# Where VectorE takes the largest of the sizes and normalizes pair 14, in a hash attention with a feed-forward behind it

## The chip, the cores and the metric

The kernel runs on one core of one Trainium2 chip. The metric is the time of one execution on the device, in microseconds (us). The kernel before took 877.48 us (median of four runs, 877.30 to 878.19).

The core has a matrix engine (TensorE, PE in the profile, its weight loads PEld), three engines for element-wise work (VectorE, DVE; ScalarE, ACT; GpSimd, POOL), and SyncE (SP), which here only issues DMAs. TensorE writes to PSUM, a small memory in banks; the rest lives in SBUF. The engines run side by side, each through its own list of instructions in order, and wait for one another by semaphores.

## The reference

Attention with a mask made from hashes, then a feed-forward block. Cut to what matters:

```python
# q, k, v: (4, 8, 768, 64) f32; proj: (64, 6); w_in: (512, 2048); w_out: (2048, 512)
q_bucket, k_bucket = bits of (q @ proj > 0), bits of (k @ proj > 0)   # 6 bits as a number
scores = where(q_bucket[..., :, None] == k_bucket[..., None, :], q @ k.T / 8, -1e9)
attn   = exp(scores - max(scores));  attn /= sum(attn) + 1e-9
x      = (attn @ v), heads side by side        # (3072, 512)
h      = x @ w_in
out    = (h * sigmoid(1.702 * h)) @ w_out      # (3072, 512)
```

## The kernel before

**Attention in 16 pairs.** Two heads form a pair, so there are 4 batches x 4 = 16 pairs, numbered 0 to 15 (`last` is 15). For each pair the 768 queries are taken in two halves c = 0 and 1 of 384. `scores(n, c, ...)` (L423) multiplies, for each of 6 tiles of 128 keys, first the hash features and then the keys with the queries (L432, tile ps), and ScalarE takes the exponential into the tile e (L433). The exponentials are taken without the largest score being subtracted first. That is only safe if q and k are not large, and so ScalarE also sums the squares of every pair's q and k (`measure`, L393) into a tile `sizes` with 32 columns. At the end of the kernel every engine loads one number, the largest of the sizes, and a branch (L981 to L984) computes everything anew in a careful way if it is too large.

`guard` (L516) makes this number, in two parts. Part 0 takes on VectorE the largest of the 32 columns in each of 128 partitions (L518). Part 1 turns that column into a row on TensorE (L521, tile row, in the PSUM buffer with the tag m) and takes the largest of the row on VectorE (L522).

**The sum under the softmax.** Each half's 6 tiles of exponentials are added up. `add_low` (L437) adds the first three on GpSimd (L440, L441) into acc0, of which there is one buffer. `add_high` (L443) adds the other three and acc0 on VectorE, by one instruction of L446 and two of L448; the last of them reads acc0. `total` (L472, tile dn) sums both halves over the partitions on TensorE. `invert` (L481) takes reciprocals on VectorE (L485 to L494) and leaves them in the tile rs. `norm` (L497) multiplies a pair's columns of xT by rs (L499), one instruction. `values` (L450, tile av) multiplies exponentials and v on TensorE, and `unload` (L466) brings the result to xT by ScalarE.

**The order.** The four computing engines run in the order in which the program is written (L72, `manual_schedule`). The loop over the pairs (L553 to L593) writes out one pair after another. An iteration n also inverts and normalizes pair n - 1, turns and hashes pair n + 1, and converts a piece of the weight w_in by 6 VectorE instructions (`step(n, 6)`, L178 to L198, with one on ScalarE, L190). In the last iteration there is no next pair: nothing is turned, hashed or measured, and the two parts of `guard` stand there instead. The last lines of the loop's body add `total(n)`, the loads of later pairs, and in the last four pairs one step each of `x_sums` (L219 to L222 on VectorE), which the feed-forward needs.

**Feed-forward in two stages.** Both multiplications are done by Strassen's scheme with 7 products in place of 8. The hidden stage (`hidden`, L698) takes 3 blocks of 1024 tokens by 8 pieces of the hidden dimension; each has 7 products of 4 matmuls (L708), in the order 1, 6, 7, 5, 2, 3, 4. Products 6, 5 and 3 use sums of quarters of w_in (tile s_in), which GpSimd makes (`in_sums`, L211 to L214, directly behind the last pair's add_low in its order). The products' banks in PSUM, six at that time, are read by ScalarE (L720) and VectorE (L721 to L733). The first block of tokens needs batch 0 and a part of batch 1; the columns of pair 14 (batch 3, third pair of heads) are used from the third block on. The hidden values go to memory and come back for the second stage (L820), whose result is turned (L800) and written out.

Of the kernel before, what the change touches and what calls it, by code (L numbers as in the profile page):

```python
# [38 lines left out]
def kernel(  # L39
# [243 lines left out]
    def attention(ff):  # L283
# [4 lines left out]
        with actx:  # L288
# [99 lines left out]
            def turn(n, name):  # L388
                x = raws[n, name]
                xt = xts[n, name] = wk.tile([P, S], F32, tag=f"{name}T", name=f"{name}T")  # L390
                nc.vector.transpose(xt, x.rearrange("p s i -> p (s i)"))
# [10 lines left out]
            def hashed(n):  # L402

                h = dots[n] = mps.tile([P, HS], F32, tag="m", name="hash")
                for i, x in enumerate("kq"):
                    for c in range(2):
                        r0 = D * i + 32 * c
                        nc.tensor.matmul(h[r0 : r0 + 32, :], pf[x], xts[n, x][:, c * HS : (c + 1) * HS],  # L408
                                         start=True, stop=True)

            def featured(n):
                f = wk.tile([P, HS], BF16, tag="f", name="f", bufs=1)
                nc.vector.tensor_scalar(f, dots.pop(n), above[:, 0:1], weight[:, 0:1], op0=Alu.is_gt, op1=Alu.mult)
                for c in range(2):
                    for i, x in enumerate("kq"):

                        queue = nc.scalar if (n, x, c) == (1, "q", 0) else nc.sync
                        for j in range(2):
                            r0 = D * i + 32 * c + 2 * NB * j
                            queue.dma_start(out=feats[n % 2][x][D * j : D * j + 2 * NB, c * HS : (c + 1) * HS],  # L420
                                            in_=f[r0 : r0 + 2 * NB, :])

            def scores(n, c, kts):  # L423
                qT, kT, qf, kf = xts[n, "q"], xts[n, "k"], feats[n % 2]["q"], feats[n % 2]["k"]
                cols = slice(c * HS, (c + 1) * HS)
                for kt in kts:
                    ps = sps.tile([P, 2, 512], F32, tag="s", name="ps")
                    keys = slice(kt * P, (kt + 1) * P)
                    for a, m, last in ((kf, qf, False), (kT, qT, True)):
                        for j in range(2):  # L430
                            hs = slice(D * j, D * (j + 1))
                            nc.tensor.matmul(ps[:, j, 0:HS], a[hs, keys], m[hs, cols], start=not last, stop=last)  # L432
                    nc.scalar.activation(es[c][:, kt, :, 0:HS], ps[:, :, 0:HS], Act.Exp, scale=1.0 / D**0.5)  # L433
# [3 lines left out]
            def add_low(n, c):  # L437

                acc = accs[n, c, 0] = st.tile([P, 2, HS], F32, tag="acc0", name="acc0", bufs=1)
                nc.gpsimd.tensor_tensor(acc, es[c][:, 0, :, 0:HS], es[c][:, 1, :, 0:HS], op=Alu.add)  # L440
                nc.gpsimd.tensor_tensor(acc, acc, es[c][:, 2, :, 0:HS], op=Alu.add)  # L441

            def add_high(n, c):  # L443
                e = [es[c][:, GT + i, :, 0:HS] for i in range(GT)]
                acc = accs[n, c] = st.tile([P, 2, HS], F32, tag="acc", name="acc")
                nc.vector.scalar_tensor_tensor(acc, e[0], T * TINY, e[1], op0=Alu.add, op1=Alu.add)  # L446
                for x in (e[2], accs.pop((n, c, 0))):
                    nc.vector.tensor_tensor(acc, acc, x, op=Alu.add)  # L448

            def values(n, c, kts):  # L450
                if 0 in kts:

                    pool, tag = (mps, "m") if c else (aps, "av")
                    avs[n, c] = pool.tile([P, HS + 1], F32, tag=tag, name="av")
                av, vt = avs[n, c], vts[n]
                for t in kts:
                    for j in range(2):
                        nc.tensor.matmul(av[D * j : D * (j + 1), :], vt[:, t, j, :], es[c][:, t, j, :],  # L458
                                         start=(t == 0), stop=(t == T - 1))

            def x_of(n):
                b, hp = pairs[n]
                x = xT[:, hp, b * S : (b + 1) * S]
                return x.rearrange("d (t p) -> d t p", p=P) if n else x.rearrange("d (p t) -> d t p", p=P)
# [7 lines left out]
            def total(n):  # L472

                dn = accs[n] = aps.tile([P, HS], F32, tag="av", name="dn")
                for c in range(2):
                    acc = accs.pop((n, c))
                    for j in range(2):
                        r0 = D * j + 32 * c
                        nc.tensor.matmul(dn[r0 : r0 + 32, :], ones[:, 0:32], acc[:, j, :], start=True, stop=True)  # L479

            def invert(n):  # L481


                rt = st.tile([P, HS // 32, 32], F32, tag="rt", name="rt", bufs=1)
                nc.vector.transpose(rt.rearrange("p s i -> p (s i)"), accs.pop(n))  # L485
                yield
                r = st.tile([P, 2, HS // 32], F32, tag="r", name="r")
                nc.vector.reciprocal(r, rt[:, :, 0].unsqueeze(1).to_broadcast([P, 2, HS // 32]))
                for r0 in range(0, P, 32):
                    c = r0 // 32 % 2  # L490
                    r1 = r0 + 32 - 64 * c
                    nc.vector.reciprocal(r[r1 : r1 + 32, c], rt[r0 : r0 + 32, :, 0])
                rs = accs[n] = st.tile([P, S], F32, tag="rs", name="rs", bufs=1)
                nc.vector.transpose(rs.rearrange("p (s i) -> p s i", i=32),  # L494
                                    r.rearrange("p c s -> p (c s)").unsqueeze(2).to_broadcast([P, S // 32, 32]))

            def norm(n):  # L497
                x, rs = x_of(n), accs.pop(n)
                nc.vector.tensor_tensor(x, x, rs.rearrange("p (t s) -> p t s", t=T), op=Alu.mult)  # L499

            last = len(pairs) - 1
            conv = {}

            def step(n, count=1):
                for _ in range(count):
                    next(conv.get(n, iter(())), None)
# [9 lines left out]
            def guard(part):  # L516
                if part == 0:
                    nc.vector.tensor_reduce(largest, sizes, axis=AX.X, op=Alu.max)  # L518
                else:
                    row = mps.tile([1, P], F32, tag="m", name="row")  # L520
                    nc.tensor.transpose(row, largest, ident)  # L521
                    nc.vector.tensor_reduce(largest[0:1, 0:1], row, axis=AX.X, op=Alu.max)  # L522
# [30 lines left out]
            for n in range(1, last + 1):  # L553
                scores(n, 0, every)
                add_low(n, 0)
                if n == 1:
                    add_high(0, 1)
                    turn(2, "k")
                    total(0)
                inverted = invert(n - 1)  # L560
                next(inverted)
                if 1 < n < last:
                    turn(n + 1, "k")
                whole(inverted)
                scores(n, 1, every)
                add_low(n, 1)
                if n < last:
                    turn(n + 1, "q")
                add_high(n, 0)
                if n < last:  # L570
                    hashed(n + 1)
                    featured(n + 1)
                    for x in "kq":
                        measure(n + 1, x)
                else:
                    guard(0)
                    guard(1)
                norm(n - 1)
                add_high(n, 1)
                values(n, 0, every)  # L580
                unload(n, 0)
                step(n, 6)
                values(n, 1, every)
                unload(n, 1)
                total(n)
                if n + 2 <= last:
                    for x in "kq":
                        fetch(n + 2, x)
                if n < last:
                    fetch_v(n + 1)  # L590
                    begin(n + 1)
                if n > last - len(x_sums):
                    x_sums[n - last - 1]()  # L593
# [378 lines left out]
    def whole(steps):  # L972
        for _ in steps:
            pass

    ff = feed_forward("", in_chunks[len(in_chunks) - LATE :])
    attention(ff)
    whole(ff)
    fixed.close()
# [41 lines left out]
```

## Time and profile before

| what | value |
|---|---|
| median of 4 runs | 877.48 us (877.30 to 878.19) |
| the profiled execution's own time | 877.48 us |
| its span, first to last instruction | 875.7 us |
| TensorE busy | 862.6 us (99%) |
| VectorE busy | 719.0 us (82%) |
| GpSimd busy | 321.3 us (37%) |
| ScalarE busy | 312.0 us (36%) |
| granted TensorE clock, mean | 0.998 |
| last pair, from its first score product to dn | 302.95 to 322.49 us |
| hidden stage | 323.3 to 611.9 us |
| second stage, TensorE's steady part | 611.9 to 850.6 us |
| behind it, to the end | 25.1 us |

All times in the views count from the first instruction of the span. A line of a timeline gives the start, the duration, the engine, the line of the program, the operation, the tile written and the tiles read; idle time before it is in brackets, with what ended it. Consecutive instructions of the same kind are merged, with x for their number. A TensorE product's end is modelled, so that successive products overlap a little. The chain is followed back from the last instruction, at each step to what released it.

### The profile page before, as it was taken

The numbers are of one execution on the slowest core, as the hardware profiler recorded it, in microseconds if no ns is written. First come the engines' busy times: TensorE is split into PE (matmuls) and PEld (weight loads), VectorE is DVE, ScalarE is ACT, GpSimd is POOL, SyncE is SP. The second block draws the span as 40 slices with busy tenths as digits, with TensorE's granted clock in tenths as the row PEclk, the third lists the DMA queues.
The fourth block names the chain that finished last, engine by engine and source line by source line (L and its number), as shares of the span: only waits on it lengthen the run. The fifth ranks groups of instructions, "written<-read, shape, count | busy, mean of one in ns | idle before, by whom it ended". The sixth has DMA issues, their size and how long they took to land.

```text
span 875.7 us, 11818 instructions
## 1 busy us (share of the span) xinstructions
PE 862.6 (99%) x4077; PEld 501.7 (57%) x4077; DVE 719.0 (82%) x1020; ACT 312.0 (36%) x519; POOL 321.3 (37%) x275
## 2 busy tenths in 40 slices
PE   9999999999999999999999999999999999999995
PEld 5444444444444444444444444444888888888884
DVE  4479999988999997788777787888888977897785
ACT  5766577777666643222232222332000000000000
POOL 4244333334433375665443344659903100000000
PEclk9999999999999999999999999999999999999999
DMA  5334456544445304555455645575844685467524
GB/s 130 61 58 84 84 97 106 117 89 83 83 84 91 74 25 144 204 204 200 166 188 190 216 166 202 191 249 171 308 164 159 199 246 198 165 202 241 193 97 99
DMA packets 169155, 131.99 MB, mean 151 GB/s; under 512 B 123616, under 2 KB 138112, under 8 KB 163712
## 3 DMA queue, kind: packets, MB, share of 16 engines
q1 hardware_dynamic: 166528, 129.70, 51.3%
q10 hardware_dynamic: 2560, 1.46, 0.7%
q8 instruction: 34, 0.56, 0.3%
q14 instruction: 33, 0.27, 0.1%
HBM read 79.69 MB, written 50.33 MB: 148 GB/s over the span
## 4 chain that ended last, share of the span: by engine, by line
PE 91%; DVE 6%; issue 1%; DMA 0%; ACT 0%; SPq 0%; ACTq 0%; DVEq 0%
PE product L708 33%; PE product L820 27%; PE ps L432 16%; PE av L458 12%; PE dn L479 1%; DVE acc L448 1%; PE hash L408 1%; DVE acc L446 1%; DVE xT L499 1%; DVE xT L824 1%; PE tp L366 1%; DVE y L800 1%; DMA q<-in_q_dram 0%; DVE t_x L221 0%; PE warm L359 0%
## 5 line engine op out<-in xcount | busy, mean ns | idle before, releaser
L433 ACT ACTIVATE e<-ps 128x768 f32<-128x768 f32 x192 | 150.4, 813 | 16.9 <-PE ps L432 14.6
L432 PE MATMUL ps<-qT,kT 64*128 64x384 f32 x768 | 155.1, 482 | 0.0
L708 PE MATMUL product<-xT,w_in_sb 128*128 128x512 f32 x288 | 135.4, 592 | 0.0
L458 PE MATMUL av<-e,v 128*64 128x385 f32 x768 | 128.2, 488 | 0.0
L440 POOL TENSOR_TENSOR acc<-e 128x768 f32<-128x768 f32 x32 | 50.4, 1575 | 192.8 <-ACT e L433 115.2
L716 ACT ACTIVATE c<-c 128x512 f32<-128x512 f32 x72 | 45.3, 630 | 186.6 <-issue 78.5
L458 PEld LDWEIGHTS av<-e,v 128*64 128x64 f32 x768 | 53.8, 136 | 72.9 <-issue 72.0
L708 PEld LDWEIGHTS product<-xT,w_in_sb 128*128 128x128 f32 x288 | 54.6, 190 | 69.0 <-issue 64.5
L708 PE MATMUL product<-t_x,s_in 128*128 128x512 f32 x192 | 90.2, 592 | 0.0
L432 PEld LDWEIGHTS ps<-qT,kT 64*128 64x128 f32 x768 | 68.1, 187 | 37.8 <-issue 37.4
L219 POOL TENSOR_TENSOR v<-c,u 128x512 f32<-128x512 f32 x24 | 34.2, 1423 | 122.8 <-ACT c L716 122.8
L833 ACT COPY u<-product 128x256 f32<-128x256 f32 x21 | 7.8, 372 | 172.1 <-PE product L820 138.9
L441 POOL TENSOR_TENSOR acc<-acc,e 128x768 f32<-128x768 f32 x32 | 64.0, 2000 | 2.5
L432 PE MATMUL ps<-qf,kf 64*128 64x384 bf16 x384 | 62.9, 324 | 0.1
L708 PEld LDWEIGHTS product<-t_x,s_in 128*128 128x128 f32 x192 | 36.5, 190 | 45.9 <-issue 43.3
L446 DVE SCALAR_TENSOR_TENSOR acc<-e 128x768 f32<-128x768 f32 x32 | 52.1, 1628 | 5.1 <-ACT e L433 5.1
L708 PE MATMUL product<-xT,s_in 128*128 128x512 f32 x96 | 45.1, 592 | 0.0
L708 PE MATMUL product<-t_x,w_in_sb 128*128 128x512 f32 x96 | 45.1, 592 | 0.0
L432 PEld LDWEIGHTS <-kf 64*128 64x128 bf16 x384 | 19.4, 94 | 35.4 <-issue 12.0
L820 PE MATMUL product<-raw_g,xT 128*128 128x256 f32 x152 | 35.1, 379 | 0.0
L448 DVE TENSOR_TENSOR acc<-acc,e 128x768 f32<-128x768 f32 x32 | 31.0, 969 | 3.8 <-ACT e L433 0.5
L448 DVE TENSOR_TENSOR acc<-acc,acc 128x768 f32<-128x768 f32 x32 | 31.0, 969 | 3.3
(207 smaller groups left out, 1495.9 us busy)
## 6 DMA issues: line engine op xcount, KB each, us to landing
raw_g<-g_dram SPq DMA_DIRECT2D x22, 1024.0 KB
s_in<-g_dram SPq DMA_DIRECT2D x20, 1024.0 KB
g_dram<-c SPq DMA_DIRECT2D x72, 256.0 KB
g_dram<-t SPq DMA_DIRECT2D x48, 256.0 KB
raw<-in_moe_w_in_dram SPq DMA_DIRECT2D x16, 512.0 KB
raw<-in_moe_w_out_dram SPq DMA_DIRECT2D x16, 512.0 KB
v<-in_v_dram SPq DMA_DIRECT2D x32, 192.0 KB
g_dram<-u SPq DMA_DIRECT2D x24, 256.0 KB
```

Source lines behind the costliest of these rows:

```text
L219: return [lambda: eng.tensor_tensor(t1, b12, b11, op=Alu.subtract), lambda: eng.tensor_tensor(b12, b22, b12, op=Alu.subtract), lambda: eng ...
L366: nc.tensor.matmul(tp[D * j : D * (j + 1), i * P : (i + 1) * P], x[name][:, j, c * GT + i, :], ident, start=True, stop=True)
L432: nc.tensor.matmul(ps[:, j, 0:HS], a[hs, keys], m[hs, cols], start=not last, stop=last)
L433: nc.scalar.activation(es[c][:, kt, :, 0:HS], ps[:, :, 0:HS], Act.Exp, scale=1.0 / D**0.5)
L440: nc.gpsimd.tensor_tensor(acc, es[c][:, 0, :, 0:HS], es[c][:, 1, :, 0:HS], op=Alu.add)
L441: nc.gpsimd.tensor_tensor(acc, acc, es[c][:, 2, :, 0:HS], op=Alu.add)
L446: nc.vector.scalar_tensor_tensor(acc, e[0], T * TINY, e[1], op0=Alu.add, op1=Alu.add)
L448: nc.vector.tensor_tensor(acc, acc, x, op=Alu.add)
L458: nc.tensor.matmul(av[D * j : D * (j + 1), :], vt[:, t, j, :], es[c][:, t, j, :], start=(t == 0), stop=(t == T - 1))
L708: nc.tensor.matmul(ps, wq[LEFT[i]][:, kc, :], xq[RIGHT[i]][:, kc, :], start=(kc == 0), stop=(kc == K2 - 1))
L716: nc.scalar.activation(c, c, Act.Gelu_apprx_sigmoid)
L820: nc.tensor.matmul(ps, wq[LEFT[i]][:, c, :], gq[RIGHT[i]][:, c, :], start=(c == 0), stop=(c == F4 - 1))
```

## The change

In the last pair's iteration alone, two steps move. `guard(0)`, VectorE's largest over the 32 columns, goes from behind the additions of the first half, add_high(15, 0), to ahead of them and ahead of the scores of the second half. `guard(1)` stays where it was. `norm(14)` goes from ahead of the additions of the second half, add_high(15, 1), to behind them. In all other iterations the order is as before.

```diff
                 whole(inverted)
+                if n == last:
+                    guard(0)
                 scores(n, 1, every)
                 add_low(n, 1)
                 if n < last:
...
                 else:
-                    guard(0)
                     guard(1)
-                norm(n - 1)
+                if n < last:
+                    norm(n - 1)
                 add_high(n, 1)
+                if n == last:
+                    norm(n - 1)
                 values(n, 0, every)
                 unload(n, 0)
                 step(n, 6)
```

VectorE's order in that iteration, before: reciprocals of pair 14, add_high(15, 0), guard(0), guard(1), norm(14), add_high(15, 1), conversion. After: reciprocals of pair 14, guard(0), add_high(15, 0), guard(1), add_high(15, 1), norm(14), conversion.

## The prediction

> **What bounds the kernel now.** I read first the page's busy shares and its chain, then the chain in order of time over the whole run, then the timeline of each engine around the two reductions that the diff moves. The first two say that TensorE is the bound nearly everywhere:
>
> ```profile
> PE 862.6 (99%) x4077; PEld 501.7 (57%) x4077; DVE 719.0 (82%) x1020; ACT 312.0 (36%) x519; POOL 321.3 (37%) x275
> PE 91%; DVE 6%; issue 1%; DMA 0%; ACT 0%; SPq 0%; ACTq 0%; DVEq 0%
> ```
>
> At 99%, a change can only give back time in which TensorE stands still, or make it stand still anew. The chain in order of time (start, duration, what) has such a place next to the edit, at the end of the last pair (pair 15):
>
> ```profile
> 264.46 9.80 PE ps L432 x72
> ...
> 314.22 0.11 DVE largest L518
> 314.37 0.27 PE row L521
> 314.64 7.92 PE av L458 x48
> 322.56 0.78 PE dn L479 x8
> 323.34 288.60 PE product L708 x672
> ```
>
> Up to 314.33 the chain is VectorE's. Then TensorE transposes the column of largest sizes (row, L521), and from there it runs to 850.6 with one hole of 0.11 us (at 689.66). What it gains at 314 it keeps for over 500 us, and the 25.1 us behind, in which VectorE, ScalarE and TensorE take turns, start from its product that ends at 850.6. TensorE's own timeline prices the place; in brackets the idle time before, and what ended it:
>
> ```profile
> 312.01 0.81 PE L432 MATMUL ps<-qT,kT 64*128 64x384 f32 x4
> 314.37 0.27 PE L521 MATMUL row<-ident,largest 128*1 128x128 f32 x1 [1.55 <-DVE largest L518]
> 314.57 7.99 PE L458 MATMUL av<-e,v 128*64 128x385 f32 x48
> 322.49 0.85 PE L479 MATMUL dn<-acc,ones 128*32 128x384 f32 x8
> 323.27 1.98 PE L708 MATMUL product<-xT,w_in_sb 128*128 128x512 f32 x4
> 325.09 1.88 PE L708 MATMUL product<-t_x,s_in 128*128 128x512 f32 x4
> ```
>
> **The change, part by part.** *guard(0) goes ahead of the last pair's additions.* It reads only the sizes. ScalarE's last one was done at 296.2, so it waits for nothing at its new place, right behind the transpose of the reciprocals (L494: 310.27 + 0.98 = 311.25), and ends near 311.4. TensorE comes to the row later than that: its first score product of pair 15 started at 302.95, and in the pairs before the scores took 9.80 (9.79 to 9.84) up to the next kind of product (first line of the second fence), so at 312.75. Its stall was 314.37 - 312.75 = **1.62 us**. The bracket says 1.55, because ends are modelled and successive products overlap by some 0.07. If the change of tile shape cost nothing, the 12 groups at 0.808 would end at 302.95 + 9.69 = 312.64, and the gain would be 1.73. I take 1.62, since all pairs show the 9.80, and keep 1.55 and 1.73 as ends.
>
> Its price: VectorE pays guard(0) (0.18 busy, 0.11 in the chain) ahead of add_high(15,0) and not behind it. I take 0.18: the third addition ends at 314.40, not 314.22. Queued behind that is GpSimd's add_low(15,1), which needs the buffer that this addition reads, and started 0.14 after it: at 314.54 now.
>
> *guard(1) keeps its place on VectorE.* The row now lies ready from 313.0, so VectorE's wait of 0.36 goes, and the reduction (0.28) runs from 314.40 to 314.68. The row's PSUM buffer is wanted again by values(15,1), at half of the 7.92 (316.9): 2.2 us of room. Nothing that is moved issues a DMA, and no step changes its place on the queues of SP, ScalarE or GpSimd.
>
> *norm(14) goes behind add_high(15,1).* VectorE's and GpSimd's timelines:
>
> ```profile
> 314.88 1.83 DVE L499 TENSOR_TENSOR xT<-xT,rs 128x768 f32<-128x768 f32 x1
> 316.64 2.43 DVE L446 SCALAR_TENSOR_TENSOR acc<-e 128x768 f32<-128x768 f32 x1
> 319.18 1.30 DVE L448 TENSOR_TENSOR acc<-acc,e 128x768 f32<-128x768 f32 x1
> 320.58 1.30 DVE L448 TENSOR_TENSOR acc<-acc,acc 128x768 f32<-128x768 f32 x1
> ...
> 314.36 1.54 POOL L440 TENSOR_TENSOR acc<-e 128x768 f32<-128x768 f32 x1 [4.37 <-DVE largest L518]
> 315.98 2.27 POOL L441 TENSOR_TENSOR acc<-acc,e 128x768 f32<-128x768 f32 x1
> 318.22 1.44 POOL L211 TENSOR_TENSOR s_in<-w_in_sb 128x256 f32<-128x256 f32 x1
> 319.74 1.32 POOL L212 TENSOR_TENSOR w_in_sb<-w_in_sb 128x256 f32<-128x256 f32 x1
> 321.03 1.44 POOL L213 TENSOR_TENSOR s_in<-s_in,w_in_sb 128x256 f32<-128x256 f32 x1
> ```
>
> These durations are long: the same L446 took 0.92 for add_high(15,0), and L448 0.96, while GpSimd was quiet, and norm(15) 0.96 where it started first. The Trainium skill (SBUF — State Buffer, "Who interferes with whom") has a rule that speaks against the move: a VectorE instruction with two SBUF inputs and a GpSimd instruction that reads SBUF can't overlap; the one that starts later stands still until the other is done. The rows agree: GpSimd's L440 ends at 315.90 and norm, started under it, at 316.71; L441 ends at 318.25 and L446 at 319.07; L211 at 319.66 and the next L448 at 320.48; L212 at 321.06 and the last L448 at 321.88. They go turn and turn about. Without the rule I would take norm's 1.83 and the 0.36 off the additions, and add the 0.18: 321.88 - 2.01 = 319.87. With it, L446 only takes norm's turn behind L440, and each VectorE turn ends as before plus 0.18: L446 at 316.89, the two L448 at 319.25 and 320.66, norm(14) at 322.06. I take the turns, since they are in the rows.
>
> What depends on it: total(15) (dn) comes forward by 1.62, to 322.49 - 1.62 = 320.87, and its second half, which reads add_high(15,1), some 0.39 later. The sum is there at 320.66: 0.2 to 0.6 us to spare, no wait. This is the cover, and it is thin: with norm still ahead, the sum would come at 321.88 + 0.18 = 322.06, 0.8 behind the second half, and half of the gain would be lost. So the two parts belong together, and the second earns nothing by itself.
>
> Late next: the first feed-forward products. Product 1 (323.27 - 1.62 = 321.65) needs nothing of this. Product 6 (325.09 - 1.62 = 323.47, weights some 0.19 ahead) needs GpSimd's L213, which ended at 322.47 and by the turns now at 322.65: 0.6 to spare. norm(14) is wanted by no product soon: its columns (batch 3, third pair of heads) belong to the last third of the hidden stage, from some 323 + 2/3 x 289 = 515 us. The conversion behind it on VectorE stays within 0.2 of its place, and behind that the sums that free PSUM: product 6 was read at 329.75, and its bank was wanted again at 335.39. The 5.6 less 0.7 for the read leave 4.9; 3.3 after the shift.
>
> **Sum.** The profiled execution took 877.48, of which its span is 875.7 and 1.8 lies around it; the median is also 877.48. -1.62 at the row, 0 at dn, 0 at product 6, nothing given back later: span 874.1, time 877.48 - 1.62 = **875.86 us (-0.18%)**. About 0.2% (1.75 us) is what a measurement of this kernel can tell from no change, so the likeliest gain lies 0.13 us inside that bound.
>
> **The clock** could make it more. The Trainium skill (TensorE: Matmul & The Clock Gate, "What's actually happening") says that the array's clock halves after about one window of 3.4 us without work. A halved clock for one window would make the old gap dearer by 1.7 us, for a total of 3.3. The stages of the windows view show 1.00 granted in the pair with the gap and in the one before, and values(15) took 7.92 as values(14) did, so I count nothing.
>
> **Rivals.**
> (a) *More than the stall.* TensorE loads the row's and the next weights while it still works on scores (the load, 0.08, came after the wait at 314.37), and the shape change is hidden: 1.73 + 0.08 = 1.8, up to 2.1 with what the tail's turns may shift: 875.4 to 875.7. For it: many weight loads run ahead. Against: the 9.80 of every pair includes such loads.
> (b) *A partial gain.* If VectorE's L446 (from 314.65) starts before GpSimd's L440 (from 314.54), the turns are exchanged: L446 ends at 315.5, L440 at 317.0, an L448 at 318.0, L441 at 319.5, L211 at 320.2, the last L448 at 321.1, L212 at 321.8, norm at 322.7, L213 at 323.4. dn just holds, and product 6's weights wait 0.1 to 0.3. With a lost turn more (0.9), the gain is 0.4 to 1.5: 876.0 to 877.1. Only 0.1 us decides which comes first.
> (c) *The hoisted reduction does nothing*, as VectorE comes to it no earlier than TensorE to the row. From 275 VectorE is on the chain, and its lead at the new place is 312.75 - 311.4 = 1.3. Should a load of q land later than the 4.1 us it took at 286.41, each us beyond the 1.3 takes one off the gain: 876 to 877.5. In this trace the lead is whole.
> (d) *Slower.* VectorE's run of two-input steps (three additions, norm, six conversion steps) keeps winning the port, and GpSimd's L213 falls behind by whole turns. Product 6 then waits. From 0.6 + 1.62 = 2.2 us of lateness on, the change loses; over 0.2% it loses from 4.0 us, about four and a half turns of 0.9, at 879.3 or more. Against it: from 314 to 323 the two engines alternate strictly in the trace.
>
> **How the numbers follow.** Full gain, 1.55 to 1.73: 0.70. Medians repeat to about 0.2 us (three of the four times lie between 877.30 and 877.50), and the bound is 0.13 away, so I put 0.36 within and 0.34 beyond it. (a): 0.12, faster. (b) and (c): 0.09, within. (d): 0.09, slower. Faster 0.46, same 0.45, slower 0.09. The range: from (a)'s 875.4, less 0.1 of scatter, to 877.0, which takes in most of (b) and (c) and leaves out (d).
>
> **What would show it.** L518 near 311.3; no idle time before the row, which starts at 312.75; guard(1) with no wait; L446 of add_high(15,1) from 314.7 with about 2.2 us, norm(14) from 320.7; dn at 320.87, the first product at 321.65, the hidden products 288.6 us as before, and a span of 874.1. A wait of TensorE for L448 at dn, or for L213 at product 6, would show (b) or (d). Idle time left before the row would show (c).

## The result, and the profile after

The changed kernel took **875.72 us** (median of 36 runs, 874.92 to 878.74), against 877.10 (median of 57, 876.07 to 878.62) for the kernel before, measured beside it. The ratio is 0.9984 with a 95% interval of 0.9979 to 0.9988: 0.16% faster, just inside the 0.2% that the prediction called the bound of a measurement. The forecast was 875.86. That the time itself fits to 0.14 us is in part luck: the forecast took its 1.62 off the 877.48 of four runs, and the kernel before, measured beside the changed one, came out at 877.10. From there 1.62 less would be 875.48; the measured gain is 1.38.

TensorE no longer stands at the row. From the changed kernel's chain in order of time (start, duration, what), over the same stretch as before:

```profile
302.74 9.80 PE ps L432 x72
312.54 0.20 PE row L521
312.74 7.92 PE av L458 x48
320.65 0.78 PE dn L479 x8
```

VectorE has disappeared from the chain here: scores, row, values and dn follow one another without a gap. TensorE's timeline, where L712 is the old L708:

```profile
312.47 0.27 PE L521 MATMUL row<-ident,largest 128*1 128x128 f32 x1
312.67 7.99 PE L458 MATMUL av<-e,v 128*64 128x385 f32 x48
320.58 0.85 PE L479 MATMUL dn<-acc,ones 128*32 128x384 f32 x8
321.37 1.99 PE L712 MATMUL product<-xT,w_in_sb 128*128 128x512 f32 x4
323.19 1.88 PE L712 MATMUL product<-t_x,s_in 128*128 128x512 f32 x4
```

There is no bracket with idle time on any of these lines. The row starts 9.80 after the pair's first score product (302.67). VectorE and GpSimd over the same stretch:

```profile
313.96 0.27 DVE L522 TENSOR_REDUCE largest<-row 1x1 f32<-1x128 f32 x1
314.17 0.94 DVE L446 SCALAR_TENSOR_TENSOR acc<-e 128x768 f32<-128x768 f32 x1
315.20 2.12 DVE L448 TENSOR_TENSOR acc<-acc,e 128x768 f32<-128x768 f32 x1
318.90 1.47 DVE L448 TENSOR_TENSOR acc<-acc,acc 128x768 f32<-128x768 f32 x1 [1.58 <-POOL acc L441]
320.29 1.48 DVE L499 TENSOR_TENSOR xT<-xT,rs 128x768 f32<-128x768 f32 x1
...
314.19 2.31 POOL L440 TENSOR_TENSOR acc<-e 128x768 f32<-128x768 f32 x1 [4.46 <-DVE acc L448]
316.58 2.28 POOL L441 TENSOR_TENSOR acc<-acc,e 128x768 f32<-128x768 f32 x1
318.82 0.73 POOL L211 TENSOR_TENSOR s_in<-w_in_sb 128x256 f32<-128x256 f32 x1
319.63 1.32 POOL L212 TENSOR_TENSOR w_in_sb<-w_in_sb 128x256 f32<-128x256 f32 x1
320.92 1.44 POOL L213 TENSOR_TENSOR s_in<-s_in,w_in_sb 128x256 f32<-128x256 f32 x1
```

The two engines still take turns, but VectorE's L446 came first by 0.02 us and ran in 0.94. It is the second addition that is held up (2.12), and VectorE then stands 1.58 for GpSimd's L441. Even so the sum is there at 318.90 + 1.47 = 320.37, ahead of dn.

To see where the time between the two profiles went, I cut each of the two profiled executions at three marks: the first score product of pair 15, the first feed-forward product, and the end of TensorE's last steady product.

| stretch | before | after | difference |
|---|---|---|---|
| start to first score product of pair 15 | 302.95 | 302.67 | -0.28 |
| pair 15, to the first feed-forward product | 20.32 | 18.70 | -1.62 |
| feed-forward, TensorE's steady part | 527.36 | 527.40 | +0.04 |
| from there to the end ("the tail") | 25.07 | 24.83 | -0.24 |
| span | 875.7 | 873.6 | -2.1 |

Pair 15 gives exactly what was forecast. The first and last rows hold nothing that the change touches; where such differences come from is told at the end.

### The profile page after: what moved, and what is told of

It reads as the page before. It is cut to its first block, busy times and chain, and to the rows that moved or that the text cites. A ratio compares the mean times of both kernels' runs of the same rounds, so it can differ in the third digit from the quotient of the medians.

```text
span 873.6 us, 11818 instructions
## 1 busy us (share of the span) xinstructions
PE 862.3 (99%) x4077; PEld 502.3 (57%) x4077; DVE 719.3 (82%) x1020; ACT 311.2 (36%) x519; POOL 321.4 (37%) x275
## 4 chain that ended last, share of the span: by engine, by line
PE 94%; DVE 4%; issue 1%; ACT 0%; ACTq 0%; DVEq 0%
PE product L712 33%; PE product L824 26%; PE ps L432 18%; PE av L458 14%; PE dn L479 1%; PE hash L408 1%; DVE y L804 1%; DVE xT L828 1%; PE tp L366 1%; DVE t_x L828 0%; DVE acc L448 0%; DVE xT L499 0%; PE warm L359 0%; PE hash L373 0%; DVE t2a L221 0%
## 5 line engine op out<-in xcount | busy, mean ns | idle before, releaser
L712 PE MATMUL product<-xT,w_in_sb 128*128 128x512 f32 x288 | 135.5, 593 | 0.0
L440 POOL TENSOR_TENSOR acc<-e 128x768 f32<-128x768 f32 x32 | 51.3, 1602 | 192.5 <-ACT e L433 114.3
L712 PEld LDWEIGHTS product<-xT,w_in_sb 128*128 128x128 f32 x288 | 54.7, 190 | 68.9 <-issue 64.2
L712 PE MATMUL product<-t_x,s_in 128*128 128x512 f32 x192 | 90.3, 593 | 0.0
L441 POOL TENSOR_TENSOR acc<-acc,e 128x768 f32<-128x768 f32 x32 | 64.1, 2002 | 2.5
L712 PEld LDWEIGHTS product<-t_x,s_in 128*128 128x128 f32 x192 | 36.5, 190 | 45.9 <-issue 43.7
L446 DVE SCALAR_TENSOR_TENSOR acc<-e 128x768 f32<-128x768 f32 x32 | 50.6, 1582 | 5.1 <-ACT e L433 5.1
L712 PE MATMUL product<-t_x,w_in_sb 128*128 128x512 f32 x96 | 45.1, 592 | 0.0
L712 PE MATMUL product<-xT,s_in 128*128 128x512 f32 x96 | 45.1, 592 | 0.0
L448 DVE TENSOR_TENSOR acc<-acc,acc 128x768 f32<-128x768 f32 x32 | 31.2, 974 | 4.8 <-POOL acc L441 1.6
L448 DVE TENSOR_TENSOR acc<-acc,e 128x768 f32<-128x768 f32 x32 | 31.8, 994 | 3.8 <-ACT e L433 0.5
```

The source lines that it names most:

```text
L712: nc.tensor.matmul(ps, wq[LEFT[i]][:, kc, :], xq[RIGHT[i]][:, kc, :], start=(kc == 0), stop=(kc == K2 - 1))
```

## The experiments

My theory: the gain is TensorE's wait at the row and nothing else; the next step to be late is dn (it needs the sum of add_high(15,1)), then product 6 (it needs GpSimd's L213). Rivals: the gain comes from VectorE's additions being earlier; or the order of turns between VectorE and GpSimd decides; or something else of the guard was on the path. The kernels of each group (e1 to e4, e5 to e7, e8 to e11) ran on one chip beside the kernel before. The diffs of e1, e4 to e7 and e9 are against the changed kernel, those of e2, e3 and e8 against the kernel before, that of e11 against e3. All results first; the two stretches are from each kernel's profiled execution:

| kernel | pair 15 | tail | median, us | ratio to before (95%) |
|---|---|---|---|---|
| before | 20.32 | 25.07 | 876.8 to 877.1 | 1 |
| the change, first time | 18.70 | 24.83 | 875.72 | 0.9984 (0.9979 to 0.9988) |
| e10, the change again | 18.69 | 24.8 | 875.59 | 0.9981 (0.9973 to 0.9989) |
| e1, guard alone | 19.41 | 24.9 | 876.08 | 0.9994 (0.9985 to 1.0002) |
| e2, norm alone | 20.35 | 25.0 | 877.16 | 1.0004 (0.9995 to 1.0012) |
| e3, row behind values | 26.41 | 24.9 | 882.69 | 1.0069 (1.0055 to 1.0083) |
| e11, the same, other bank | 19.24 | 25.1 | 875.87 | 0.9985 (0.9979 to 0.9991) |
| e4, no guard | 18.50 | 24.8 | 874.38 | 0.9971 (0.9959 to 0.9982) |
| e5, GpSimd first | 18.69 | 24.0 | 874.79 | 0.9973 (0.9963 to 0.9983) |
| e6, GpSimd late | 19.05 + 0.53 | 24.0 | 875.42 | 0.9983 (0.9976 to 0.9990) |
| e7, no row on TensorE | 18.49 | 24.0 | 874.42 | 0.9972 (0.9961 to 0.9982) |
| e8, before, three steps more | 20.30 | 24.1 | 876.34 | 0.9993 (0.9985 to 1.0001) |
| e9, the change, three steps more | 18.69 | 24.0 | 874.39 | 0.9970 (0.9958 to 0.9982) |

**e1: the guard alone.**

```diff
                 else:
                     guard(1)
-                if n < last:
-                    norm(n - 1)
+                norm(n - 1)
                 add_high(n, 1)
-                if n == last:
-                    norm(n - 1)
```

> guard(0) ahead of add_high(15,0) as in the change, but norm(14) stays ahead of add_high(15,1). Theory of the turns (two engines alternate at SBUF, and the sum for dn is the next thing to be late): no wait at the row, but the last addition ends 0.9 to 1.7 us later than in the changed kernel, so TensorE stands at dn for 0.3 to 1.1 us; gain against before 0.5 to 1.3 us, time about 876.0 to 876.5 where before is 877.1 and the full change 875.7. Rival (only the row's wait ever counted, dn has cover enough): no idle time at dn, the full gain of 1.4 to 1.6 us.

TensorE's, VectorE's and GpSimd's timelines of e1:

```profile
313.08 0.27 PE L521 MATMUL row<-ident,largest 128*1 128x128 f32 x1
321.20 1.57 PE L479 MATMUL dn<-acc,ones 128*32 128x384 f32 x8
...
314.81 0.94 DVE L499 TENSOR_TENSOR xT<-xT,rs 128x768 f32<-128x768 f32 x1
315.68 0.94 DVE L446 SCALAR_TENSOR_TENSOR acc<-e 128x768 f32<-128x768 f32 x1
...
320.42 1.46 DVE L448 TENSOR_TENSOR acc<-acc,acc 128x768 f32<-128x768 f32 x1 [1.57 <-POOL acc L441]
...
314.84 3.18 POOL L440 TENSOR_TENSOR acc<-e 128x768 f32<-128x768 f32 x1 [4.46 <-DVE acc L448]
```

The row doesn't wait, but dn takes 1.57 in place of 0.85: its second half stands until the sum is there at 321.88. Pair 15 takes 19.41, which is 0.91 less than before and 0.71 more than with the whole change. The median (0.69 under before) fits that, though its interval still reaches 1. The theory holds; the rival, that dn has cover enough, falls. The turns were not as I had drawn them, though: norm(14) (L499) and L446 ran one behind the other, both ahead of GpSimd's L440, which therefore took 3.18. Why GpSimd got no turn between the two is open.

**e2: the normalization alone.** Both parts of the guard stay as before, norm(14) goes behind add_high(15,1).

```diff
-                norm(n - 1)
+                if n < last:
+                    norm(n - 1)
                 add_high(n, 1)
+                if n == last:
+                    norm(n - 1)
```

> norm(14) goes behind add_high(15,1), both parts of the guard stay where they were before. Theory (TensorE's wait for the guard is the whole of it): the row still waits about 1.55 us, the sums for dn come 1 to 1.5 us earlier and nobody uses it; ratio 1.000, within 0.2 us of before. Rival (VectorE's additions, which the chain runs through ahead of dn, are what counts): a gain of 0.5 us or more.

Pair 15 takes 20.35, no less than before; the row waits 1.60; the ratio is 1.0004 with 1 in its interval. The sum is there at 320.41 in place of 321.88, and nobody uses it. So the rival that earlier additions themselves are worth something falls.

**e3 and e11: TensorE comes to the row later.** Here guard(0) stays at its old place. The row and guard(1) go behind values(15,0), where TensorE arrives some 4 us later; norm(14) is moved as in the change.

```diff
                 else:
                     guard(0)
-                    guard(1)
...
                 values(n, 0, every)
+                if n == last:
+                    guard(1)
                 unload(n, 0)
```

> guard(0) stays at its old place behind add_high(15,0); the row's transpose and guard(1) go behind values(15,0), so that TensorE comes to the row some 4 us later; norm(14) goes behind add_high(15,1). Theory (what counts is that TensorE doesn't wait at the row, not where VectorE does the reduction): no idle time at the row, dn in time, gain 1.4 to 1.7 us as the change has, 875.5 to 875.8. Rival (the gain comes from the reduction leaving VectorE's stretch between the additions): under 0.5 us.

I missed, and lost 6 us. The row itself doesn't wait, but the product behind it does (e3, TensorE):

```profile
311.97 4.10 PE L458 MATMUL av<-e,v 128*64 128x385 f32 x24
316.00 0.27 PE L521 MATMUL row<-ident,largest 128*1 128x128 f32 x1
321.55 6.33 PE L458 MATMUL av<-e,v 128*64 128x385 f32 x24 [5.27 <-DVE largest L522]
```

values(15,1) writes to the PSUM buffer that the row occupies. What frees it is guard(1)'s reduction, and that now lies behind norm(14) on VectorE (321.22). The same cover is 2.2 us wide in the change, where guard(1) comes early; I had priced it there and not for this kernel.

The wait is not the whole loss. The 24 matmuls behind it took 6.33, where the same number ahead of it took 4.10. The trace's record of the granted clock has full speed up to 319.25, half from there to 326.08, and full speed again. So TensorE, idle from 316.2, was put to half its clock some 3 us later, and the half clock cost 2.2 us on top of the wait. Wait and clock together come to some 7.5; the old stall of 1.6, now gone, is to be taken from that, and pair 15 takes 26.41 against 20.32.

So e11 moves the row alone to another bank:

```diff
-                    row = mps.tile([1, P], F32, tag="m", name="row")
+                    row = sps.tile([P, 2, 512], F32, tag="s", name="row")[0:1, 0, 0:P]
```

> As e3 (guard(0) at its old place, row and guard(1) behind values(15,0), norm(14) behind add_high(15,1)), but the row goes into a PSUM buffer of the scores, which nobody needs until the feed-forward. In e3 values(15,1) stood 5.3 us for the buffer that VectorE's guard(1) frees. Theory (only TensorE's waits count, not the place of the reduction): without that wait pair 15 takes 18.7 to 18.9 us to the first feed-forward product and the gain is the change's, 1.4 to 1.7 us, unless the product that reuses this bank waits for guard(1), up to 0.5 us. Rival (the hoist itself is needed): under 0.7 us of gain.

Pair 15 takes 19.24. Of that, 0.33 is a wait of the first feed-forward product, which reuses the bank, for guard(1). The rest above 18.70, some 0.2, is for the most part TensorE's: the row now splits the values in two (4.03 and 4.04 between starts, for 7.92 in one piece). The ratio is 0.9985, the change's within the intervals. So the gain doesn't need guard(0) to be hoisted, which lies here where it lay before; it is enough that TensorE doesn't come to the row too early.

**e4: no guard at all.** The check on the sizes is left out: `largest` is set to zero at the start. Otherwise as the change.

```diff
+    later.append((largest, 0.0))
...
-                if n == last:
-                    guard(0)
...
-                else:
-                    guard(1)
```

> The guard is left out: largest is set to zero at the start, no reduction and no row; norm(14) behind add_high(15,1). An upper bound for any placing of the guard. Theory: the stall of 1.62 goes and with it the 0.20 that the row takes on TensorE: dn 1.8 us earlier than before after the pair's first score product, 875.3 where before is 877.1. If more than 2.0 us go, something else of the guard was on the path (the rival: code or queue effects); if under 1.5, dn or the first products wait.

18.50 for pair 15: the row's 0.20 and nothing more. The change has thus taken out all of the guard's price except the row's own time. The median, at 2.39 under the kernel before, lies lower than these 1.82 explain; with 7 runs of this kernel and an interval of 0.23% I don't read the rest.

**e5: GpSimd first.** Since VectorE had won the first turn by 0.02 us, three more reductions on VectorE reverse the order.

```diff
                     guard(1)
+                    spare = st.tile([P, 1], F32, tag="spare", name="spare", bufs=1)
+                    for _ in range(3):
+                        nc.vector.tensor_reduce(spare, sizes, axis=AX.X, op=Alu.max)
```

> The changed kernel with three more reductions over the sizes on VectorE ahead of add_high(15,1), together 0.3 to 0.5 us, so that GpSimd's add_low(15,1) starts first and VectorE's first addition second. Theory of the turns: L440 1.54 us, L446 2.0 us or more, the last addition ends 0.2 to 0.7 us later than in the changed kernel, at most at the moment when dn's second half begins; no or under 0.3 us idle time at dn; time as the changed kernel within 0.3 us. Rival (the order decides over the time): 0.9 us or more lost.

VectorE and GpSimd in e5:

```profile
314.69 1.86 DVE L446 SCALAR_TENSOR_TENSOR acc<-e 128x768 f32<-128x768 f32 x1
316.66 2.25 DVE L448 TENSOR_TENSOR acc<-acc,e 128x768 f32<-128x768 f32 x1
319.01 1.30 DVE L448 TENSOR_TENSOR acc<-acc,acc 128x768 f32<-128x768 f32 x1
...
314.20 1.54 POOL L440 TENSOR_TENSOR acc<-e 128x768 f32<-128x768 f32 x1 [4.46 <-DVE acc L448]
```

These are the turns that the prediction had drawn: L440 free, L446 held up, then one after the other. The sum comes at 319.01 + 1.30 = 320.31, no later than with VectorE first (320.37), and pair 15 takes 18.69. Which engine goes first makes no difference here: with VectorE first, VectorE waits for L441 instead. I had expected a delay of 0.2 to 0.7, so that half of the expectation missed; that the time of pair 15 stays held. The median, 0.9 under the changed kernel's, is taken up below.

**e6: GpSimd late.** One more addition on GpSimd ahead of the sums of w_in.

```diff
+            spare = st.tile([P, S], BF16, tag="junk", name="junk", bufs=1)[:, 0:512]
+            nc.gpsimd.tensor_tensor(spare, w_in_sb[:, 0, 0:512], w_in_sb[:, 1, 0:512], op=Alu.add)
             for f in in_sums(0):
                 f()
```

> The changed kernel with one more addition of 128x512 on GpSimd ahead of the sums of w_in (1.3 us alone, up to 2 against VectorE), result unused. If the first feed-forward product that reads s_in (product 6) is the next thing to be late, with 0.6 to 0.8 us to spare, TensorE stands there for 0.5 to 1.6 us and the time is that much above the changed kernel's. Rival (the slack is larger, or VectorE gives up turns): no idle time at product 6, the time of the changed kernel.

TensorE and GpSimd in e6 (L714 is the old L708, L599 the addition put in):

```profile
320.20 1.21 PE L479 MATMUL dn<-acc,ones 128*32 128x384 f32 x8
321.34 1.99 PE L714 MATMUL product<-xT,w_in_sb 128*128 128x512 f32 x4
323.69 1.55 PE L714 MATMUL product<-t_x,s_in 128*128 128x512 f32 x3 [0.37 <-POOL s_in L213]
...
318.43 1.26 POOL L599 TENSOR_TENSOR junk<-w_in_sb 128x512 bf16<-128x512 f32 x1
322.47 1.17 POOL L213 TENSOR_TENSOR s_in<-s_in,w_in_sb 128x256 f32<-128x256 f32 x1
```

Product 6 waits for L213: it starts 2.35 after product 1 where 1.82 is the rule, so 0.53 are lost. That product 6 is the next to be late, with some 0.6 to spare, holds. Another 0.36 is lost at dn (1.21 for 0.85), which I had not expected: the addition put in is longer than the sums' first step, and it is VectorE's last L448 (2.02) that stands behind it. The time (875.42) is not above the changed kernel's, which would contradict the 0.89 if the tail did not show 0.8 less.

**e7: no row on TensorE.** VectorE takes the largest over the partitions alone, behind norm(14).

```diff
-                    row = mps.tile([1, P], F32, tag="m", name="row")
-                    nc.tensor.transpose(row, largest, ident)
-                    nc.vector.tensor_reduce(largest[0:1, 0:1], row, axis=AX.X, op=Alu.max)
+                    row = st.tile([P, S], BF16, tag="junk", name="junk", bufs=1).bitcast(F32)[0:32, 0:P]
+                    for r0 in range(0, P, 32):
+                        nc.vector.transpose(row[:, r0 : r0 + 32], largest[r0 : r0 + 32].to_broadcast([32, 32]))
+                    nc.vector.tensor_reduce(largest[0:1, 0:1], row[0:1], axis=AX.X, op=Alu.max)
...
-                else:
-                    guard(1)
...
                 if n == last:
                     norm(n - 1)
+                    guard(1)
```

> The changed kernel, but the largest over the partitions is taken by VectorE alone: four transposes of 32x32 and one reduction, behind norm(14); TensorE has no row. Theory: TensorE is spared the 0.20 us of the row and nothing else: values(15) follows the scores at once, 0.2 us less than the changed kernel in the profile (875.5), too little to be told from it by the times. Rival: the five VectorE steps (0.7 to 1 us) push the conversion behind them, the first sums or the first reads of PSUM, and TensorE waits in the hidden stage: slower than the changed kernel by 0.3 us or more.

18.49 for pair 15, as without any guard, while everything is computed: the five VectorE steps (1.1 us) lie ahead of the conversion and delay nothing. With 0.9972 it beats both kernels, but only 0.2 of its lead on the changed kernel is explained by the row.

**e8, e9 and e10: the tail.** e5, e6 and e7 ended 24.0 us after TensorE's last steady product, all others so far 24.8 or more. What the three share is that they have two or three instructions more (11,820 or 11,821 against 11,815 to 11,818). So three reductions went behind norm(15), into a stretch where VectorE waits for TensorE: once into the kernel before (e8), once into the changed one (e9), with the changed kernel beside them (e10).

```diff
             norm(last)
+            spare = st.tile([P, 1], F32, tag="spare", name="spare", bufs=1)
+            for _ in range(3):
+                nc.vector.tensor_reduce(spare, sizes, axis=AX.X, op=Alu.max)
```

> The kernel before, with three short reductions of the sizes on VectorE behind norm(15), result unused, in a stretch where VectorE waits for TensorE anyway. In e5, e6 and e7, which have two or three instructions more than the changed kernel, the part behind TensorE's last steady product took 24.0 us; in the kernels without them 24.8 to 25.1. If the length of the program decides over that part (which code the engines still have to fetch at the branch at the end), this kernel has 24.0 there and is 0.8 to 1.0 us faster than before though it does more. Rival (scatter of single executions): 24.8 to 25.1, ratio 1.000.

> The changed kernel with the same three reductions behind norm(15). By the length of the program: 24.0 behind the last steady product and 0.8 to 1.0 us under the changed kernel, about 874.8. Rival (scatter; or only e5's place mattered): as the changed kernel, 875.7.

> The changed kernel again, beside the others on one chip. Pair 15 from its first score product to the first feed-forward product 18.7 us, against 20.3 before; part behind the last steady product 24.8; 1.4 to 1.6 us under before.

The tail is 24.1 in e8, 24.0 in e9 and 24.8 in e10. By the medians e8 is 0.79 under the kernel before (the interval just reaches 1), e9 is 1.2 under e10. The DMA view of the stretch from 845 to 890 us, which reaches beyond the end of the span, counts the transfers of code (queue, kind: packets, MB, share). First the changed kernel, then e9:

```profile
q14 instruction: 6, 0.05, 0.3%
```

```profile
q14 instruction: 5, 0.04, 0.2%
```

In all 13 profiles six such transfers go with a tail of 24.8 to 25.1, and five with 24.0 to 24.1. But the sixth is a sign and not the cause: in each of the eight profiles it starts 0.3 to 0.7 us after the last instruction has ended, so nothing in the span can wait for it.

Where the time goes is in the trace's records of semaphore instructions, which the views leave out. At the very end the engines meet twice. In the kernel before, SyncE, ScalarE and TensorE go on from the first meeting at 874.17, and VectorE only at 875.33; the span ends at 875.68. In e8 all four go on at 873.74. Sorted by the number of VectorE's instructions:

| VectorE's instructions | kernels | VectorE behind the others |
|---|---|---|
| 1435 | e4 | 0.7, at the second meeting |
| 1437 | before, the change, e1, e2, e3, e10, e11 | 1.0 to 1.2, at the first meeting |
| 1438 to 1441 | e5, e6, e7, e8, e9 | none (up to 0.02) |

The counts of the other engines don't sort them so: e4 and e6, on different sides, both have one instruction more on GpSimd, e11 has one more on TensorE, and ScalarE and SyncE have the same number in all. In all eight late kernels the late step is the same by its place: the 1435th of the instructions that the trace has of VectorE. So it is the length of VectorE's own list that moves the tail, by what stands at one place of that list. That VectorE waits there for its next piece of code is inferred: in each of the eight the fifth transfer above falls into the wait and ends 0.4 to 0.8 us ahead of VectorE's step.

## Why the prediction was right

**The stall at the row.** Forecast 1.62, taken from the row's start against 9.80 after the first score product, and not the 1.55 of the bracket. The row now starts at 302.67 + 9.80, and pair 15 is 1.62 shorter (18.69 in e10, 1.63). Nothing of it was given back: the steady part of the feed-forward took 527.4 in both profiles.

**guard(0)'s own price.** I charged 0.18; from L494's start to L446's it is 0.97 for 0.91 before, so 0.06. guard(1) ran at once, as forecast.

**The turns.** This step failed, as rival (b) had warned: I let GpSimd's L440 go first, and VectorE was there 0.02 us sooner. Both set out from the end of the third addition (313.09 + 0.96 = 314.05). GpSimd started 0.14 behind it, as forecast; VectorE, with guard(1) in between, started L446 0.12 behind it, where I had reckoned 0.25. But (b)'s price was wrong too. It had the sum at 321.1 and L213 at 323.4; they came at 320.37 and 322.36. L446 ended 0.4 us earlier than (b) has it, most of which (0.28) had come in ahead of pair 15, and each turn behind it took a little under 0.1 us less than the durations alone, from which (b) is built. e5 ran the order I had forecast and ended in the same place. That one engine stands while the other has its turn held in the traces of this pair: in the changed kernel L440 ends 1.4 after L446's end (it takes 1.54 alone), and the second addition 0.8 after L440's (0.96 alone). That the turns always alternate did not: in e1 VectorE had two in a row.

**The cover at dn.** Forecast 0.2 to 0.6 to spare; the sum was there 0.21 ahead of dn and some 0.6 ahead of its second half. Without the move of norm(14) I put the loss at 0.8; e1 lost 0.71. The size fits, but in part by luck, since the turns of e1 were not the ones I had reckoned with. That this move earns nothing by itself, e2 shows.

**What is late next.** L213 was forecast 0.6 ahead of product 6's weights: 323.19 - 0.19 - 322.36 = 0.64. e6 made it late.

**The clock.** The granted clock, the third figure from the end of a line, stays 1.00 in this pair, with and without the gap (the windows views of the kernel before and of the changed one):

```profile
302.95:323.27 20.32, 18.77 (x134) 8.96 (x130) 19.16 (x24) 11.27 (x17) 12.76 (x8) 1.00 0.09 27
302.67:321.37 18.70, 18.70 (x134) 9.03 (x130) 16.46 (x22) 11.23 (x17) 11.11 (x7) 1.00 0.10 29
```

The prediction's 1.7 us for a halved clock is an estimate, half of the window that it cites, and counting nothing for it was right here: a gap of 1.55 left the clock at 1.00. e3 shows the other case: after a gap of 5.27 TensorE ran on at half its clock until 326.08, and lost another 2.2 us.

**The size.** The medians differ by 1.38, the second time (e10) by 1.54, with intervals of about 0.4 and 0.7 us on either side, against 1.62 in pair 15. Rival (a) would have needed the row to start sooner than 9.80 behind the scores; it didn't. (c) and (d) left no trace: no idle time at the row, none at dn, none at product 6.

## What to carry to other kernels

A small step that hands work from one engine to another can cost far more than it takes: 0.18 us on VectorE held TensorE for 1.62, because it stood behind additions that it did not need. Once such a step is hoisted, look at once for what its consumer reaches next; here the sum for dn had 0.2 us, and nearly half of the gain hung on moving a normalization that nobody was waiting for. And before a step that writes to a shared buffer is moved, find who frees it: e3 lost 6 us to a PSUM buffer whose reader lay at the wrong place in VectorE's order, 2.2 of them by the lower clock that the wait brought on.

## What the runs showed of the hardware that I had not expected

The end of this kernel depends on how long VectorE's list of instructions is. Three reductions whose results nobody reads shortened the tail by 0.8 to 0.9 us (25.07 to 24.1 in e8, 24.8 to 24.0 in e9), because VectorE was no longer late where the engines meet at the end. That is half of what the change itself earned, so kernels that differ by a few instructions can't be compared to better than this unless the tail is looked at separately. The Trainium skill (Runtime: NRT & Kernel Launch, "Instruction fetch mechanics") says that code comes in blocks of 16 KiB and is hidden by the pace of issue; the page of the kernel before has 0.56 MB in 34 packets on one of the two queues, about 16 KB each, but 0.27 MB in 33 packets on the other, about 8 KB each. If VectorE's wait at the end is one for code, as inferred above, not all of it is hidden.

Executions also differ in their beginning: the first score product of pair 15 lay between 301.98 and 303.29 us in the 13 profiles, in no relation to the edits. Most of this is there after 11 us: the first score product of all lay between 10.06 and 11.21, though TensorE's first transposes began at 3.65 to 3.86 in every profile. It goes along with the clock, for which the traces record full speed from a moment between 4.98 and 8.42 us on; by and large, the later that is, the later the first score product. Only the stretch of pair 15 itself, which repeats to 0.01 us (18.69, 18.69, 18.69 and 18.70 in four kernels that have the same order on TensorE), could settle differences of 0.2.
